# Moving the V loads of five batches from the SP queue to the ACT queue in a fused attention and feed-forward kernel

## The chip, the cores and the metric

The kernel runs on one core of a Trainium2 chip. The metric is the device time of one execution in microseconds (us). Each execution also lists its span and the mean granted TensorE clock (1.0 is full speed). The engines are PE (TensorE), DVE (VectorE), ACT (ScalarE), POOL (GpSimd) and SP (SyncE). "SPq" and "ACTq" in the profile are the instruction streams in which SP and ACT issue their DMAs.

## The reference, cut to what matters

```python
# q, k, v: (8 batches, 8 heads, 576 tokens, 64), f32
scores = scale * q @ k.T                       # per batch and head
mask   = (pos_q - pos_k >= 0) & (pos_q - pos_k < 64)   # causal window of 64
x      = softmax(where(mask, scores, -1e9)) @ v
x      = x.transpose(0, 2, 1, 3).reshape(4608, 512)
h      = x @ w_in                              # 512 -> 2048
g      = h * clip(h + 3, 0, 6) / 6             # hardswish
out    = g @ w_out                             # 2048 -> 512, f32
```

## The kernel before: the parts that matter

The 4608 tokens are handled in nine blocks, T0 to T8, of 512. A block has a first product (x times w_in, then a ReLU on ACT and a multiply on DVE, which make `gT`) and a second product (`gT` times w_out). The attention of batch T+1 is interleaved with the second product of block T. A batch also needs DMAs: loads of q, k and V, two transposing DMAs that make `QKT` (which I call the QKT transposes), and four that make `xT` (the x transposes). All of them, and the stores, are issued by SP:

```python
def load_v(b):                       # five DMAs: four of 256 KB, a tail of 128 KB, rows of 256 bytes
    ...
        nc.sync.dma_start(out=st, in_=v[b, h0 : h0 + nh, kb * P : kb * P + ss, :].rearrange("h s d -> s h d"))
    ...                              # POOL casts each piece to bf16
def load_nat(b):                     # batches 2 to 7
    ...
    nc.sync.dma_start_transpose(out=QK_tiles[...]..., in_=n[:]...)      # QKT <- nat, twice per batch
    ...
    for it in load_v(b):             # V follows q and k, on SP
        yield from it
...
    nc.sync.dma_start_transpose(out=xT[:, g, ...], in_=cell["o"][:]...) # xT <- opg, four per batch
```

The first product has three PSUM slots. A slot is free again when ACT and DVE have read it:

```python
for c in range(NCH):                              # eight chunks of two 128-column groups
    hT = two_banks([("g", T, c)])                 # waits until the DVE multiply of an earlier chunk is done
    ...matmuls into hT...
    nc.scalar.activation(out=t1[:], in_=hT[:], func=RELU, bias=half[:], scale=1.0 / 6.0)
    nc.vector.scalar_tensor_tensor(out=gT[...], in0=t1, scalar=1.0, in1=hT[:], op0=MIN, op1=MULT)
```

The matmuls beside which a unit of attention is put are given by a table (`S` is scores, `PV` is probabilities times V):

```python
REST = ((4, "S", 0), (11, "S", 1), (18, "S", 2), (19, "PV", 0), (25, "S", 3), (26, "PV", 1),
        (33, "PV", 2), (41, "PV", 3))
```

The softmax here doesn't subtract the row's maximum and nothing guards it: scores larger than these inputs give would overflow.

## Time and profile before

317.3 us, median of three runs (317.08 to 318.01). The profiled run has a span of 316.7 us.

The first lines are from the page of the kernel before: the busy table (us, share of the span, instructions), the DMA queues (packets, MB, share of 16 engines), and the DMA issues (KB each, median us from issue to landing).

```profile
PE 300.6 (95%) x2494; PEld 158.1 (50%) x2531; DVE 171.6 (54%) x201; ACT 165.4 (52%) x220; POOL 93.0 (29%) x133
...
q1 hardware_dynamic: 152784, 57.95, 84.4%
...
st<-in_v_dram SPq DMA_DIRECT2D x28, 256.0 KB, 5.0
...
QKT<-nat SPq DMA_TRANSPOSE x12, 5.5
```

PE is busy nearly all the time. One queue, SP's, carries 57.95 of the 58.35 MB.

Where PE is not busy after the opening, the view of waits tells why (us in total, times, longest):

```profile
PE ps L638 <- DMA xT<-opg: 1.9, 3, 0.7
```

L638 is the first product; it waits for x transposes. The windows view compares block T2, which has no such wait, with T4 (window, PE busy, PEld, DVE, ACT, POOL busy, then granted clock, DMA share, GB/s). Blocks are counted in this document from their first matmul of the first product:

```profile
94.13:126.24 32.11, 31.79 (x237) 15.80 (x240) 18.73 (x20) 17.80 (x24) 11.03 (x15) 1.00 1.14 205
158.51:192.20 33.69, 32.05 (x236) 15.82 (x240) 18.41 (x20) 17.80 (x24) 10.33 (x15) 1.00 0.99 197
```

T4 is 1.58 us longer, with about the same work. The timelines of SP and of PE around its start (start us, us, engine, line, operation, out<-in, count, then idle time before and its releaser) show the cause:

```profile
152.00 2.60 SPq L590 DMA_TRANSPOSE xT<-opg  x2
154.69 0.53 SPq L702 DMA_DIRECT2D out_dram<-osb  x1
155.32 3.98 SPq L590 DMA_TRANSPOSE xT<-opg  x2
...
160.02 6.52 SPq L374 DMA_TRANSPOSE QKT<-nat  x2
```

```profile
158.51 0.59 PE L638 MATMUL ps<-xT,win 128*128 128x512 bf16 x2
159.79 0.38 PE L638 MATMUL ps<-xT,win 128*128 128x512 bf16 x1 [0.69 <-DMA xT<-opg]
160.74 0.81 PE L638 MATMUL ps<-xT,win 128*128 128x512 bf16 x2 [0.58 <-DMA xT<-opg]
```

The last x transposes leave SP only at 155 to 159 us, and the first product wants them from 158.5 us.

### The profile page before, as it was taken

How to read it: one execution, taken by the hardware profiler on the slowest of the kernel's cores; microseconds unless marked ns; L12 is line 12 of the kernel's file. 1: busy time of each engine (PE TensorE's matmuls, PEld its weight loads, DVE VectorE, ACT ScalarE, POOL GpSimd, SP SyncE). 2: the span in 40 equal slices, each digit the busy share in tenths (PEclk: the TensorE clock that was granted, in tenths of full speed). 3: DMA queues.
4: the chain of work that ended last, by engine and by line, in shares of the span. 5: the costliest groups of instructions: out<-in, count | busy, mean ns of one | idle time of the engine just before them, and what ended most of it. 6: DMA issues, size and time to landing. Idle time of an engine off the chain costs nothing.

```text
span 316.7 us, 6130 instructions
## 1 busy us (share of the span) xinstructions
PE 300.6 (95%) x2494; PEld 158.1 (50%) x2531; DVE 171.6 (54%) x201; ACT 165.4 (52%) x220; POOL 93.0 (29%) x133
## 2 busy tenths in 40 slices
PE   6889979999999999999989999999999999999994
PEld 2554345544544455875534454445575544444442
DVE  5676568656825783477337751767166716404700
ACT  5655557367715771667146833683368336316511
POOL 3258738413730363037301640066003000000000
PEclk9999999999999999999999999999999999999998
DMA  8999999999999999999999989999993430010011
GB/s 212 240 370 386 386 307 214 235 214 209 211 202 196 218 214 192 198 207 214 178 184 221 202 188 165 240 206 197 204 213 58 126 91 0 33 68 33 0 68 67
DMA packets 152813, 58.35 MB, mean 184 GB/s; under 512 B 142032, under 2 KB 142032, under 8 KB 152784
## 3 DMA queue, kind: packets, MB, share of 16 engines
q1 hardware_dynamic: 152784, 57.95, 84.4%
q8 instruction: 20, 0.33, 0.4%
q14 instruction: 9, 0.07, 0.1%
HBM read 36.70 MB, written 9.44 MB: 146 GB/s over the span
## 4 chain that ended last, share of the span: by engine, by line
PE 77%; DMA 12%; SPq 6%; issue 1%; POOL 1%; DVE 0%; ACT 0%; ACTq 0%
PE ps L638 35%; PE acc L682 34%; DMA st<-in_moe_w_in_dram 4%; PE ps L528 4%; DMA st<-in_v_dram 3%; DMA st<-in_k_dram 3%; SPq L354 3%; PE ps L565 3%; PE ps L570 2%; DMA xT<-opg 2%; SPq L590 1%; SPq L316 1%; POOL V L261 1%; POOL win L261 1%; PE ps L607 0%
## 5 line engine op out<-in xcount | busy, mean ns | idle before, releaser
L650 DVE SCALAR_TENSOR_TENSOR gT<-t,ps 128x1024 bf16<-128x1024 bf16 x72 | 87.9, 1221 | 94.1 <-ACT t L647 94.1
L682 PE MATMUL acc<-wout,gT 128*128 128x512 bf16 x550 | 131.5, 379 | 2.3 <-issue 0.8
L638 PE MATMUL ps<-xT,win 128*128 128x512 bf16 (+4 forms) x693 | 126.1, 340 | 2.5 <-DMA xT<-opg 1.9
L647 ACT ACTIVATE t<-ps,half 128x1024 bf16<-128x1024 f32 x72 | 80.2, 1114 | 52.2 <-PE ps L638 52.2
L638 PEld LDWEIGHTS <-win 128*128 128x128 bf16 x704 | 65.2, 98 | 62.1 <-issue 2.9
L682 PEld LDWEIGHTS <-gT 128*128 128x128 bf16 x576 | 52.8, 98 | 58.5 <-issue 1.1
L699 ACT COPY osb<-acc 128x512 f32<-128x512 f32 x36 | 21.2, 590 | 69.6 <-PE acc L682 65.6
L537 ACT ACTIVATE pT<-ps 128x768 bf16<-128x768 f32 x64 | 48.6, 809 | 10.7 <-PE ps L528 10.4
L261 POOL CAST V<-st 128x512 bf16<-128x512 f32 (+1 forms) x30 | 19.4, 648 | 112.2 <-DMA st<-in_v_dram 108.8
L261 POOL CAST nat<-st 128x512 bf16<-128x512 f32 x48 | 37.3, 781 | 20.6 <-DMA st<-in_k_dram 11.7
L548 DVE TENSOR_TENSOR pT<-pT,mask 128x1920 bf16<-128x1920 bf16 x28 | 34.4, 1228 | 8.7 <-ACT pT L543 8.7
L583 DVE TENSOR_TENSOR opg<-ps,rec 128x640 bf16<-128x640 f32 x32 | 26.4, 825 | 1.1
L565 PEld LDWEIGHTS <-pT 128*128 128x128 bf16 x320 | 20.6, 98 | 5.3 <-DVE pT L548 0.2
L565 PE MATMUL ps<-V,pT 128*128 128x65 bf16 x320 | 22.0, 194 | 0.5 <-issue 0.3
L570 PE MATMUL ps<-V,pT 128*128 128x65 bf16 x256 | 20.9, 193 | 0.0
L528 PEld LDWEIGHTS <-QKT 64*128 64x128 bf16 x320 | 11.4, 94 | 14.4 <-issue 11.6
L570 PEld LDWEIGHTS <-pT 128*128 128x128 bf16 x256 | 17.9, 98 | 0.3 <-issue 0.3
L528 PE MATMUL ps<-QKT 64*128 64x192 bf16 (+1 forms) x320 | 17.7, 234 | 0.0
L580 DVE RECIPROCAL rec<-ps 128x10 f32<-128x10 f32 x32 | 7.0, 218 | 12.4 <-PE ps L570 12.1
L497 PE MATMUL ps<-ident,run 64*64 64x64 bf16 x288 | 6.7, 194 | 4.6 <-DVE run L258 2.8
L258 DVE CAST run<-st 128x576 bf16<-128x576 f32 x13 | 6.1, 473 | 8.1 <-DMA st<-in_q_dram 6.0
L261 POOL CAST nat<-tl 64x512 bf16<-64x512 f32 x12 | 9.3, 776 | 3.0 <-DMA tl<-in_q_dram 2.5
(46 smaller groups left out, 83.8 us busy)
## 6 DMA issues: line engine op xcount, KB each, us to landing
out_dram<-osb SPq DMA_DIRECT2D x36, 256.0 KB, 2.7
st<-in_v_dram SPq DMA_DIRECT2D x28, 256.0 KB, 5.0
st<-in_q_dram SPq DMA_DIRECT2D x24, 256.0 KB, 5.3
st<-in_k_dram SPq DMA_DIRECT2D x24, 256.0 KB, 5.4
st<-in_moe_w_in_dram SPq DMA_DIRECT2D x4, 1024.0 KB, 10.0
st<-in_moe_w_out_dram SPq DMA_DIRECT2D x4, 1024.0 KB, 14.8
st<-in_q_dram SPq DMA_DIRECT2D x8, 288.0 KB, 6.6
st<-in_k_dram SPq DMA_DIRECT2D x8, 288.0 KB, 5.8
```

Source lines behind the costliest of these rows:

```text
L261: return lambda s: nc.gpsimd.tensor_copy(out=out_ap, in_=in_ap) and None
L528: nc.tensor.matmul(st[:, h, off : off + w], lhsT=KT[h * D : (h + 1) * D, kb * P : (kb + 1) * P], rhs=QT[h * D : (h + 1) * D, kb * P : kb * ...
L537: nc.scalar.activation(out=pT[:, :, kbs[0] : kbs[0] + 2, 0:QW], in_=st[:, :, 0 : 2 * QW].rearrange("p h (k w) -> p h k w", k=2), func=EXP, ...
L548: pl.op("DVE", t, 1.2, lambda s: nc.vector.tensor_tensor(out=pT[:, :, :, 0:QW], in0=pT[:, :, :, 0:QW], in1=mask[:].rearrange("p (h k) w -> ...
L565: nc.tensor.matmul(ob, lhsT=pT[:, h, qb, 0:P], rhs=V[:, qb, 2 * g + h, :], start=True, stop=(qb == 0),)
L570: nc.tensor.matmul(ob, lhsT=pT[:, h, qb - 1, P : 2 * P], rhs=V[:, qb - 1, 2 * g + h, :], start=False, stop=True,)
L583: nc.vector.tensor_tensor(out=opg[:].rearrange("p k h d -> p h k d"), in0=ov[:, :, :, 0:D], in1=rec[:].unsqueeze(3).to_broadcast([P, 2, KB ...
L638: nc.tensor.matmul(hT[:, j, dst : dst + w], lhsT=win16[:, g, fc * P : (fc + 1) * P], rhs=xT[:, g, src : src + w], start=(g == 0), stop=(g ...
L647: nc.scalar.activation(out=t1[:], in_=hT[:], func=RELU, bias=half[:], scale=1.0 / 6.0)
L650: nc.vector.scalar_tensor_tensor(out=gT[:, 2 * c : 2 * c + 2, :], in0=cell["t"][:], scalar=1.0, in1=hT[:], op0=MIN, op1=MULT,)
L682: nc.tensor.matmul(accs[ts], lhsT=gT[:, fc, ts * P : (ts + 1) * P], rhs=wout16[:, fc, :], start=(fc == 0), stop=(fc == NFC - 1),)
L699: nc.scalar.copy(out=osb[:], in_=acc)
```

## The change

Its intent: take the five V loads of each of the batches 3 to 7 off SP, so that SP reaches the x transposes earlier. They go to ACT, spaced between its ReLUs, with a staging buffer of their own (`vstage`, `vtail`). That costs one of the six common staging buffers and one of three buffers for tails. The diff has more than that: it also rewrites the opening (order of loads and of attention units of batch 0, casts of the weights), takes the PV units earlier, and lets the first chunk of a block take its last x group last. Its core:

```diff
-NSTAGE = 6
+NSTAGE = 5
+VGAP = 1.4
+VISSUE = 0.6
...
+def stream_v(b):
+    def issue(kb):
+        def fn(s):
+            ...
+            nc.scalar.dma_start(
+                out=st.rearrange("p (h d) -> p h d", h=H),
+                in_=v[b, :, kb * P : kb * P + ss, :].rearrange("h s d -> s h d"))
+            ...
+            if kb < KB - 1:
+                pl.op("ACT", s + VGAP, VISSUE, issue(kb + 1))
+        return fn
+    gate = (("pv", b - 2, NG - 1), ("x", b - 1, NG - 1))   # in the plan, behind the x transposes of the batch ahead
+    pl.op("ACT", 0.0, VISSUE, issue(0), deps=gate)
...
 def load_nat(b):
     ...
-    for it in load_v(b):
-        yield from it
...
+        if c == 0:        # first chunk: the last x group last
+            order.sort(key=lambda x: x[2] == NG - 1 and x[1] is parts[-1])
...
-REST = ((4, "S", 0), (11, "S", 1), (18, "S", 2), (19, "PV", 0), (25, "S", 3), (26, "PV", 1),
-        (33, "PV", 2), (41, "PV", 3))
+REST = ((4, "S", 0), (10, "S", 1), (16, "S", 2), (17, "PV", 0), (22, "S", 3), (23, "PV", 1),
+        (29, "PV", 2), (36, "PV", 3))
... (opening: ORDER, MERGE, load_v_halves, split of the first w_in tile)
```

`pl` is a plan that is made when the program is built: it only sets the order of the instructions on each engine.

More of the change, by code (lines that the diff above doesn't have):

```diff
@@ L25 @@
 NEG = -30000.0
-QK_ENG = ([('ACT',), ('DVE',), ('ACT',), ('DVE',)], (("DVE", "ACT"),) * 4)
-X_ENG = ([('DVE', 'ACT'), ('DVE', 'ACT'), ('ACT',), ('DVE',)], (("DVE", "ACT"),) * 4)
+QK_ENG = ((('DVE', 'ACT'), ('ACT',), ('ACT',), ('ACT',)), (("DVE", "ACT"),) * 4)
+MERGE = ('ppppvvvppvpvpvvvvv', "ppppppvpvpvvv")
+ORDER = (('T', 0), ('T', 1), ('S0', 0), ('S1', 0), ('S1', 1), ('T', 2), ('S0', 1), ('PV', 0), ('S1', 2), ('T', 3), ('S0', 2), ('PV', 1), ('S1', 3), ('PV', 2), ('S0', 3), ('X', 0), ('PV', 3), ('X', 2), ('X', 1), ('X', 3))
+X_ENG = ((('DVE',), ('DVE', 'ACT'), ('DVE',), ('DVE', 'ACT')), (("DVE", "ACT"),) * 4)
 NWARM = 11
-PRIO = lambda g, f: ({"S0": 0, "S1": 0, "T": 1, "PV": 2, "X": 3}[f], g)
 class Plan:
@@ L137 @@
     stage = ctx.enter_context(tc.tile_pool(name="stage", bufs=NSTAGE))
-    tails = ctx.enter_context(tc.tile_pool(name="tails", bufs=3))
+    tails = ctx.enter_context(tc.tile_pool(name="tails", bufs=2))
+    vstage = ctx.enter_context(tc.tile_pool(name="vstage", bufs=1))
+    vtail = ctx.enter_context(tc.tile_pool(name="vtail", bufs=1))
     small = ctx.enter_context(tc.tile_pool(name="small", bufs=3))
@@ L187 @@
     P_ring = [consts.tile([P, 2, KB, 2 * P], BF16, name=f"pT{i}") for i in range(NPT)]
-    V_ring = [consts.tile([P, KB, H, VW], BF16, name=f"V{i}") for i in range(2)]
+    V_ring = [consts.tile([P, NG, KB, 2, VW], BF16, name=f"V{i}") for i in range(2)]
     nc.vector.memset(idle[:], 0.0)
@@ L234 @@
     for i, t in enumerate(V_ring):
-        at("POOL", 2.0 + 14 * i, 0.3, lambda t=t: nc.gpsimd.memset(t[:, :, :, D:VW], 1.0))
-        at("POOL", 2.2 + 14 * i, 0.9, zero("POOL", t[D:P, KB - 1, :, 0:D]), ("Vz", i))
+        at("POOL", 2.0 + 14 * i, 0.3, lambda t=t: nc.gpsimd.memset(t[:, :, :, :, D:VW], 1.0))
+        at("POOL", 2.2 + 14 * i, 0.9, zero("POOL", t[D:P, :, KB - 1, :, 0:D]), ("Vz", i))
     for t in natural:
         at("POOL", 17.0, 0.6, zero("POOL", t[S % P : P, :, KB - 1, :]))
-    dma = {"t": 2.4}
+    dma = {"t": 2.2, "lag": 0.2}
     DEPTH = 4.0
@@ L252, in moved @@
         dma["t"] = max(dma["t"], now) + kb / rate
-        land = dma["t"] + 1.9
+        land = dma["t"] + 1.9 + dma["lag"]
         return max(now + 0.06, dma["t"] - 5.0), land
@@ L281, in load_items @@
             if b < NR6:
-                yield from load_pairs(b)
+                ps, vs = load_pairs(b), load_v_halves(b) if b == 0 else load_v(b)
+                for c in MERGE[b]:
+                    yield next(ps if c == "p" else vs)
             else:
                 yield from load_nat(b)
+                if b == NR6:
+                    yield from load_v(b)
             if b == 0:
@@ L301, in tail_slot @@
         tail_hist.append(casts)
-        return tuple(tail_hist[-4]) if len(tail_hist) > 3 else ()
+        return tuple(tail_hist[-3]) if len(tail_hist) > 2 else ()
     def load_pairs(b):
-        vs = load_v(b)
         for gg in range(0, NG, 2):
@@ L319, in go @@
                         )
-                        fr, land = moved(s, 295, 385)
+                        fr, land = moved(s, 295, 385 if b else 330)
                         casts(("cast", b, i, g), land, [
@@ L324, in load_pairs @@
                     yield b, deps[i], go
-            if b == 0:
-                yield from next(vs)
-        for it in vs:
-            yield from it
     def load_v(b):
@@ L333, in load_v @@
         tiles = {}
-        nh = 4 if b == 0 else H
-        deps = stage_slot([("cast", b, 2, i, h0) for i in range(KB - 1) for h0 in range(0, H, nh)])
-        if b >= 2:
-            deps += (("pv", b - 2, NG - 1),)
-        if b == 2:
-            deps += (("issued", b, 1),)
-        if b > 2:
-            deps += (("s1v", b - 1),)
-        tdeps = tail_slot([("cast", b, 2, KB - 1, h0) for h0 in range(0, H, nh)])
-        for h0 in range(0, H, nh):
-            its = []
+        deps = stage_slot([("cast", b, 2, i) for i in range(KB - 1)])
@@ new lines, in load_v, with go @@
+        if b >= NR6:
+            deps += (("pv", b - 2, NG - 1), ("issued", b, 1))
+        tdeps = tail_slot([("cast", b, 2, KB - 1)])
+        for kb in range(KB):
+            ss = min(P, S - kb * P)
+            def go(s, kb=kb, ss=ss):
+                if kb == 0:
+                    tiles["t"] = stage.tile([P, 4, H * D], F32, name="st", tag="st")
+                if kb == KB - 1:
+                    st = tails.tile([P, H * D], F32, name="tl", tag="tl")[:ss, :]
+                else:
+                    st = tiles["t"][:, kb, :]
+                nc.sync.dma_start(
+                    out=st.rearrange("p (h d) -> p h d", h=H),
+                    in_=v[b, :, kb * P : kb * P + ss, :].rearrange("h s d -> s h d"),
+                )
+                fr, land = moved(s, 262 * ss / P, 205)
+                casts(("cast", b, 2, kb), land, [(
+                    ("POOL",), V[:ss, :, kb, :, 0:D], st.rearrange("p (g h d) -> p g h d", g=NG, h=2), H * D)])
+                return fr
+            yield b, deps + tdeps if kb == KB - 1 else deps, go
@@ new lines, in stream_v @@
+    def stream_v(b):
+        V = V_ring[b % 2]
+        tiles = {}
+        def issue(kb):
+            ss = min(P, S - kb * P)
+            def fn(s):
+                if kb == 0:
+                    tiles["t"] = vstage.tile([P, 4, H * D], F32, name="sv", tag="sv")
+                if kb == KB - 1:
+                    st = vtail.tile([P, H * D], F32, name="tv", tag="tv")[:ss, :]
+                else:
+                    st = tiles["t"][:, kb, :]
+                nc.scalar.dma_start(
+                    out=st.rearrange("p (h d) -> p h d", h=H),
+                    in_=v[b, :, kb * P : kb * P + ss, :].rearrange("h s d -> s h d"),
+                )
+                _, land = moved(s, 262 * ss / P, 205)
+                casts(("cast", b, 2, kb), land, [(
+                    ("POOL",), V[:ss, :, kb, :, 0:D], st.rearrange("p (g h d) -> p g h d", g=NG, h=2), H * D)])
+                if kb < KB - 1:
+                    pl.op("ACT", s + VGAP, VISSUE, issue(kb + 1))
+            return fn
+        gate = (("pv", b - 2, NG - 1), ("x", b - 1, NG - 1))
+        if b > NR6 + 1:
+            gate += tuple(("cast", b - 1, 2, kb) for kb in range(KB))
+        pl.op("ACT", 0.0, VISSUE, issue(0), deps=gate)
@@ L345, in load_v, with load_v_halves, go @@
+    def load_v_halves(b):
+        V = V_ring[b % 2]
+        tiles = {}
+        deps = stage_slot([("cast", b, 2, i, kb) for i in range(2) for kb in range(KB - 1)])
+        tdeps = tail_slot([("cast", b, 2, i, KB - 1) for i in range(2)])
+        for i in range(2):
             for kb in range(KB):
                 ss = min(P, S - kb * P)
-                def go(s, kb=kb, ss=ss, h0=h0):
-                    if "t" not in tiles:
-                        tiles["t"] = stage.tile([P, 4, H * D], F32, name="st", tag="st")
-                    if kb == KB - 1 and "l" not in tiles:
-                        tiles["l"] = tails.tile([P, H * D], F32, name="tl", tag="tl")
-                    st = tiles["l"][:ss, :] if kb == KB - 1 else tiles["t"][:, kb, :]
-                    st = st[:, h0 * D : (h0 + nh) * D].rearrange("p (h d) -> p h d", h=nh)
+                def go(s, i=i, kb=kb, ss=ss):
+                    if not tiles:
+                        tiles["t"] = stage.tile([P, 2, 4, 4 * D], F32, name="st", tag="st")
+                        tiles["l"] = tails.tile([P, 2, 4 * D], F32, name="tl", tag="tl")
+                    st = tiles["l"][:ss, i, :] if kb == KB - 1 else tiles["t"][:, i, kb, :]
@@ L354, in go @@
                     nc.sync.dma_start(
-                        out=st,
-                        in_=v[b, h0 : h0 + nh, kb * P : kb * P + ss, :].rearrange("h s d -> s h d"),
-                    )
-                    fr, land = moved(s, 262 * ss / P * nh / H, 200)
-                    eng = ("DVE", "ACT", "POOL") if b == 0 else ("POOL",)
-                    casts(("cast", b, 2, kb, h0), land, [(eng, V[:ss, kb, h0 : h0 + nh, 0:D], st, nh * D)])
-                    return fr
-                its.append((b, deps + tdeps if kb == KB - 1 else deps, go))
@@ L363, in load_v @@
-            yield its
+                        out=st.rearrange("p (h d) -> p h d", h=4),
+                        in_=v[b, 4 * i : 4 * i + 4, kb * P : kb * P + ss, :].rearrange("h s d -> s h d"),
+                    )
+                    fr, land = moved(s, 131 * ss / P, 200)
+                    casts(("cast", b, 2, i, kb), land, [(
+                        ("DVE", "ACT", "POOL"), V[:ss, 2 * i : 2 * i + 2, kb, :, 0:D],
+                        st.rearrange("p (g h d) -> p g h d", g=2, h=2), 4 * D)])
@@ L365, in load_nat @@
+                    return fr
+                yield b, deps + tdeps if kb == KB - 1 else deps, go
     def load_nat(b):
@@ L408, in load_nat, with go @@
                 yield b, deps + tail_slot([("cast", b, i, kb)]) if kb == KB - 1 else deps, go
-        for it in load_v(b):
-            yield from it
     WC = FF // 4
     def load_w():
+        dma["lag"] = 0.8
         for i in range(4):
             deps = stage_slot([("win", i, 0), ("win", i, 1)])
-            def go(s, i=i):
-                st = stage.tile([P, NG, WC], F32, name="st", tag="st")
-                nc.sync.dma_start(
-                    out=st[:],
-                    in_=moe_w_in[:, i * WC : (i + 1) * WC].rearrange("(g p) f -> p g f", p=P),
-                )
-                fr, land = moved(s, 1049, 388)
-                for hf in range(2):
-                    casts(("win", i, hf), land, [(
-                        ("POOL",), win16[:, 2 * hf : 2 * hf + 2, i * WC : (i + 1) * WC],
-                        st[:, 2 * hf : 2 * hf + 2, :], 1024)])
-                return fr
-            yield 0, deps, go
+            n = 2 if i == 0 else 1
+            tiles = {}
+            for j in range(n):
+                def go(s, i=i, j=j, n=n, tiles=tiles):
+                    w, w2 = WC // n, WC // 2
+                    if not tiles:
+                        tiles["t"] = stage.tile([P, n, NG, w], F32, name="st", tag="st")
+                    st = tiles["t"][:, j]
+                    nc.sync.dma_start(
+                        out=st, in_=moe_w_in[:, i * WC + j * w : i * WC + (j + 1) * w].rearrange("(g p) f -> p g f", p=P),
+                    )
+                    fr, land = moved(s, 1049 / n, 388 if n == 1 else 350)
+                    for hf in range(2) if n == 1 else (j,):
+                        c0 = i * WC + hf * w2
+                        casts(("win", i, hf), land, [(
+                            ("POOL",) if i else ("DVE", "ACT", "POOL"), win16[:, :, c0 : c0 + w2],
+                            st[:, :, hf * w2 : (hf + 1) * w2] if n == 1 else st, NG * w2)])
+                    return fr
+                yield 0, deps, go
         for i in range(4):
@@ L474, in ready @@
         elif f == "PV":
-            ks = [soft(b, g)] + vcasts(b, g)
+            ks = soft(b, g) + vcasts(b, g)
         else:
@@ L481, in soft @@
     def soft(b, g):
-        return ("mask", b, g) if b else ("exp", b, g, 1)
+        return [("mask", b, g)] if b else [("exp", b, g, i) for i in range(2)]
     def vcasts(b, g):
-        nh = 4 if b == 0 else H
-        return [("cast", b, 2, kb, 2 * g // nh * nh) for kb in range(KB)]
+        return [("cast", b, 2, g // 2, kb) for kb in range(KB)] if b == 0 else [("cast", b, 2, kb) for kb in range(KB)]
     def tqk(b, g):
@@ L556, in pv @@
     def pv(b, g):
-        for r in [soft(b, g)] + vcasts(b, g):
+        for r in soft(b, g) + vcasts(b, g):
             pl.wait(r)
@@ L565, in pv @@
                 nc.tensor.matmul(
-                    ob, lhsT=pT[:, h, qb, 0:P], rhs=V[:, qb, 2 * g + h, :],
+                    ob, lhsT=pT[:, h, qb, 0:P], rhs=V[:, g, qb, h, :],
                     start=True, stop=(qb == 0),
@@ L570, in pv @@
                     nc.tensor.matmul(
-                        ob, lhsT=pT[:, h, qb - 1, P : 2 * P], rhs=V[:, qb - 1, 2 * g + h, :],
+                        ob, lhsT=pT[:, h, qb - 1, P : 2 * P], rhs=V[:, g, qb - 1, h, :],
                         start=False, stop=True,
@@ L629, in s1 @@
         for c in range(NCH):
-            if T == 0 and c % 2 == 0:
-                pl.wait(("win", c // 2, 0))
-                pl.wait(("win", c // 2, 1))
+            if T == 0:
+                pl.wait(("win", c // 2, c % 2))
             hT = two_banks([("g", T, c)])
-            for j in range(2):
-                fc = 2 * c + j
-                for dst, src, w in parts:
-                    for g in range(NG):
-                        nc.tensor.matmul(
-                            hT[:, j, dst : dst + w], lhsT=win16[:, g, fc * P : (fc + 1) * P],
-                            rhs=xT[:, g, src : src + w], start=(g == 0), stop=(g == NG - 1),
-                        )
-                pl.pe(4 * 0.216)
+            order = [(j, p, g) for j in range(2) for p in parts for g in range(NG)]
+            if c == 0:
+                order.sort(key=lambda x: x[2] == NG - 1 and x[1] is parts[-1])
+            for j, (dst, src, w), g in order:
+                nc.tensor.matmul(
+                    hT[:, j, dst : dst + w], lhsT=win16[:, g, (2 * c + j) * P : (2 * c + j + 1) * P],
+                    rhs=xT[:, g, src : src + w], start=(g == 0), stop=(g == NG - 1),
+                )
+                pl.pe(0.216 * w / TB)
             cell = {}
@@ L711 @@
     next_load(0.0)
+    for b in range(NR6 + 1, B):
+        stream_v(b)
     warm = two_banks(["warm"])
@@ L728, in unit @@
             xt(b, g, cells.pop((b, g)))
-    todo = {g: ["T", "S0", "S1", "PV", "X"] for g in range(NG)}
-    while any(todo.values()):
-        for g, f in sorted(((g, u[0]) for g, u in todo.items() if u), key=lambda x: PRIO(*x)):
-            if ready(f, 0, g):
-                todo[g].pop(0)
-                unit(f, 0, g)
-                break
-        else:
-            pl.pe(0.05)
+    for f, g in ORDER:
+        unit(f, 0, g)
     for r in held.pop():
```

## The prediction

> **What bounds the kernel now.** TensorE: 300.6 of 316.7 us busy (busy table), 77% of the chain of waits. By the windows view, a 512-token block with attention beside it (T1 from 62.2 us, T2 from 94.3) takes 32.1 us with 31.7 busy; nothing can be won there. The loss is elsewhere:
> - T3 and T4 take 33.4 and 33.2 us. The timeline shows TensorE waiting for "DMA xT<-opg": 0.69 + 0.57 us from 159.1, 0.63 at 193.0. SP's timeline shows why: SP is full all block: two QKT transposes 6.6 us, five V loads 5.5, q 5.7, k 5.5 to 7.2, stores, four x transposes of 1.2. In T3 the k loads end at 151.2 us and the x transposes issue only from 152.0 to 159.3 (one took 2.66 us).
> - The opening (0 to 62.2 us) has about 8 us of TensorE idle: 5 before the first feed-forward matmul at 22.5 us, 3 in T0, of which 0.4 for a w_out cast and 1.6 for the first q/k casts of batch 1. From 16 to 40 us DMA moves about 386 GB/s (slices), so T0's weights and the q/k after them come no earlier.
>
> **What the change does** (the diff has more than its title).
> 1. For batches 3 to 7, V's issues (5.5 us) leave SP for ACT. SP gets slack, so x transposes no longer stand behind k. The bytes stay. [...]
> 2. A block's last PV moves from the 42nd to the 37th matmul of the second product: 5 x 0.216 = 1.1 us more for the x transposes; the first chunk also takes its last x group last. Estimate: the 1.9 us of x stalls go, and 0.5 of small slips.
> 3. In T0, 22 rather than 14 second-product matmuls precede batch 1's transposes: 8 x 0.216 = 1.7 us of waiting filled. The opening is reordered and the first w_in tile split: 0.3 to 1 us by estimate, partly lost again in a longer wait for w_out. One staging buffer fewer may delay batch 1's k and V by 1 us.
> 4. Added: 25 ACT issues, 0.57 us each [...], three per block between ReLUs. ReLU 1.11 + 0.57 = 1.68 us, just under a chunk's 1.73 us: no stall. At 1.1 us [...] ACT falls 0.5 us behind per chunk, mostly absorbed by three PSUM slots.
>
> **Prediction.** 317.3 - 2.4 (T3, T4) - 1.9 (opening) + 0.3 (ACT) = 313.3 us; 310.8 to 316.8. Faster by over 2%: 0.13; within: 0.79; slower: 0.08.
>
> **What would show it.** T3 and T4 near 32.1 us without waits for xT; SP free before x; ACT's issues near 0.6 us, ReLU not late; T0 ending near 60 us; T1, T2 unchanged.
>
> **What would make it wrong.** ACT held in its issue: [...] V now falls beside the QKT transposes, 3.3 us each on SP. If ACT waited that long, five blocks would lose 1 to 3 us each. Or V, sharing bandwidth, lands too late for PV.

The 0.216 us of a matmul is a first product without waits, 13.81 us, over its 64 matmuls. The 0.57 us and the 1.1 us of an ACT issue were estimates from V's issues on SP in the trace before: their median is 0.58 us there, and from T1 on they take 0.40 to 2.07 us, 0.95 in the mean. (The five of a block take 4.4 to 5.2 us there, not 5.5.)

The prediction counts its blocks from a slightly later point: the waits at 159.1 and 193.0 us, which it puts into T3 and T4, stand in this document at the starts of T4 and T5.

## The result, and the profile after

The changed kernel takes **328.73 us** (median of 4 runs, 326.47 to 330.39), the kernel before 317.43 us in the same rounds. The ratio is 1.0349, with a 95% interval of 1.0283 to 1.0416: slower by 3.5%. Executions over 1.5% slower than the fastest of the same kernel are left out of the means. A ratio here and below is the mean time of one kernel's fast runs over that of the other's of the same rounds, so it is not quite the ratio of the medians that are quoted. The prediction of 313.3 us (310.8 to 316.8) was wrong.

The page of the kernel after, the same parts:

```profile
PE 306.8 (94%) x2531; PEld 158.8 (49%) x2531; DVE 172.1 (53%) x204; ACT 164.9 (51%) x218; POOL 91.0 (28%) x132
...
q1 hardware_dynamic: 129872, 52.05, 72.9%
q10 hardware_dynamic: 23440, 5.90, 9.6%
...
sv<-in_v_dram ACTq DMA_DIRECT2D x20, 256.0 KB, 5.3
...
QKT<-nat SPq DMA_TRANSPOSE x12, 9.0
```

V is on its own queue (q10). V lands nearly as fast as before, but a QKT transpose now lands after 9.0 us instead of 5.5.

The starts of the first products, from the PE timelines of both profiled runs, tell where the time came from:

| block | before: start, length us | after: start, length us | difference |
|---|---|---|---|
| opening and T0 | 0, 62.03 | 0, 63.52 | +1.49 |
| T1 | 62.03, 32.10 | 63.52, 32.14 | +0.04 |
| T2 | 94.13, 32.11 | 95.66, 34.92 | +2.81 |
| T3 | 126.24, 32.27 | 130.58, 36.28 | +4.01 |
| T4 | 158.51, 33.69 | 166.86, 33.45 | -0.24 |
| T5 | 192.20, 32.89 | 200.31, 34.70 | +1.81 |
| T6 to the last matmul | 225.09, 87.69 | 235.01, 87.69 | 0.00 |

Of the 9.9 us, 1.5 lie in the opening and T0. The rest lies in T2, T3 and T5, and in T4 a new loss has taken the place of the old one; all of this is in the first products. PE's waits after (only the two that matter here; L690 is the first product now):

```profile
PE ps L690 <- DVE gT L702: 5.8, 3, 2.4
PE ps L690 <- DMA xT<-opg: 2.3, 3, 1.3
```

The first wait did not exist before: PE finds no free PSUM slot, because a ReLU and so the DVE multiply behind it are late. It occurs in T3, T4 and T5. ACT's timeline at the start of T3 shows the late ReLU. The lines are, in order: V's third and fourth piece, two ReLUs, V's tail, three ReLUs.

```profile
130.85 0.37 ACTq L374 DMA_DIRECT2D sv<-in_v_dram  x1
...
132.53 0.37 ACTq L374 DMA_DIRECT2D sv<-in_v_dram  x1
134.27 1.11 ACT L699 ACTIVATE t<-ps,half 128x1024 bf16<-128x1024 f32 x1 [0.63 <-PE ps L690]
138.57 0.61 ACTq L374 DMA_DIRECT2D tv<-in_v_dram  x1
139.23 3.13 ACT L699 ACTIVATE t<-ps,half 128x1024 bf16<-128x1024 f32 x3 [3.84 <-DMA QKT<-nat]
```

The issues themselves are cheap: 0.37 us, and beside the ReLU. But nothing starts on ACT between 134.27 and 138.57 us, and what ended the idle time is "DMA QKT<-nat", a transposing DMA on the *other* queue. SP and PE at the same time:

```profile
128.38 10.23 SPq L423 DMA_TRANSPOSE QKT<-nat  x2
```

```profile
130.58 8.90 PE L690 MATMUL ps<-xT,win 128*128 128x192 bf16 x80
141.65 4.53 PE L690 MATMUL ps<-xT,win 128*128 128x192 bf16 x25 [2.18 <-DVE gT L702]
```

PE goes on until its three slots are full, stalls for 2.2 us, and resumes when the third chunk's ReLU and multiply are done. The records of line L374 from 126 to 142 us (duration in ns: minimum, median, maximum; then the first and last start) hold the wait itself:

```profile
L374 ACTq EVENT_SEMAPHORE  x3: 17/38/4251, 127.3 to 134.3; - x3
L374 ACTq DMA_DIRECT2D tv<-in_v_dram x1: 614/614/614, 138.6 to 138.6; - x1
```

A semaphore wait of 4.25 us in ACT's stream, the last of three, from 134.3 to 138.6 us: that is the gap. The wait is a record of its own, and the tail's record, 0.61 us long, follows it. So ACT waited here for a semaphore. It was not held within its issue, which is what I had named as my main worry.

T3 lost 4.0 us, but its stall was 2.2. The rest is the clock. The windows view (the third number from the end is the granted clock):

```profile
142.00:144.00 2.00, 2.00 (x14) 1.47 (x12) 1.86 (x2) 0.36 (x1) 0.61 (x1) 0.63 1.20 289
144.00:146.00 2.00, 2.00 (x11) 1.39 (x10) 0.39 (x1) 1.11 (x1) 0.72 (x2) 0.52 1.37 218
146.00:148.00 2.00, 2.00 (x21) 1.70 (x20) 0.83 (x1) 0.99 (x1) 1.11 (x2) 1.00 1.37 217
```

Right after the stall the trace has a clock record of 0.50 from 142.52 us, 3.41 us long: by estimate from the windows, 2 x (1 - 0.63) + 2 x (1 - 0.52) = 1.7 us more. So PE's busy time rose by more than the work did (a part of the rise in the busy table is only that the trace before lacks 37 of 2531 matmul records).

### The profile page after: what moved, and what is told of

Its sections match the earlier page's. It is cut to its first block, busy times and chain, and to the rows that moved or that the text cites. A ratio compares the mean times of both kernels' runs of the same rounds, so it can differ in the third digit from the quotient of the medians.

```text
span 326.5 us, 6180 instructions
## 1 busy us (share of the span) xinstructions
PE 306.8 (94%) x2531; PEld 158.8 (49%) x2531; DVE 172.1 (53%) x204; ACT 164.9 (51%) x218; POOL 91.0 (28%) x132
## 2 busy tenths in 40 slices
DMA packets 153341, 58.35 MB, mean 179 GB/s; under 512 B 142048, under 2 KB 143072, under 8 KB 153312
## 4 chain that ended last, share of the span: by engine, by line
PE 72%; DMA 20%; SPq 2%; POOL 2%; DVE 2%; ACT 1%; issue 1%; ACTq 0%; POOLq 0%
PE acc L734 34%; PE ps L690 29%; PE ps L581 4%; DMA st<-in_moe_w_out_dram 4%; DMA st<-in_moe_w_in_dram 3%; DMA sv<-in_v_dram 3%; DMA st<-in_k_dram 3%; DMA QKT<-nat 3%; PE ps L618 3%; PE ps L623 2%; DMA tl<-in_v_dram 2%; DVE gT L702 1%; DMA xT<-opg 1%; ACT t L699 1%; SPq L351 1%; POOL wout L266 1%
## 5 line engine op out<-in xcount | busy, mean ns | idle before, releaser
L734 PE MATMUL acc<-wout,gT 128*128 128x512 bf16 x576 | 136.9, 380 | 1.9 <-POOL wout L266 1.5
L690 PE MATMUL ps<-xT,win 128*128 128x512 bf16 (+4 forms) x704 | 128.9, 344 | 8.2 <-DVE gT L702 5.8
L690 PEld LDWEIGHTS <-win 128*128 128x128 bf16 x704 | 66.1, 99 | 69.7 <-issue 9.7
L266 POOL CAST nat<-st 128x512 bf16<-128x512 f32 x48 | 34.8, 729 | 25.2 <-DMA st<-in_q_dram 15.7
L601 DVE TENSOR_TENSOR pT<-pT,mask 128x1920 bf16<-128x1920 bf16 x28 | 35.5, 1269 | 6.4 <-ACT pT L596 6.4
L266 POOL CAST V<-sv 128x512 bf16<-128x512 f32 x20 | 12.4, 619 | 73.7 <-DMA sv<-in_v_dram 71.2
L263 DVE CAST run<-st 128x576 bf16<-128x576 f32 x15 | 7.6, 515 | 10.8 <-DMA st<-in_q_dram 6.2
L265 ACT COPY QKT<-ps 128x1152 bf16<-128x1152 bf16 x6 | 6.8, 1129 | 11.2 <-PE ps L550 11.2
L266 POOL CAST V<-st 128x512 bf16<-128x512 f32 (+1 forms) x10 | 6.2, 626 | 21.3 <-DMA st<-in_v_dram 21.3
L266 POOL CAST nat<-tl 64x512 bf16<-64x512 f32 x12 | 10.9, 910 | 1.5 <-DMA tl<-in_q_dram 0.8
```

Source lines behind the costliest of these rows:

```text
L266: return lambda s: nc.gpsimd.tensor_copy(out=out_ap, in_=in_ap) and None
L601: pl.op("DVE", t, 1.2, lambda s: nc.vector.tensor_tensor(out=pT[:, :, :, 0:QW], in0=pT[:, :, :, 0:QW], in1=mask[:].rearrange("p (h k) w -> ...
L690: nc.tensor.matmul(hT[:, j, dst : dst + w], lhsT=win16[:, g, (2 * c + j) * P : (2 * c + j + 1) * P], rhs=xT[:, g, src : src + w], start=(g ...
L734: nc.tensor.matmul(accs[ts], lhsT=gT[:, fc, ts * P : (ts + 1) * P], rhs=wout16[:, fc, :], start=(fc == 0), stop=(fc == NFC - 1),)
```

## Why ACT waits: the theory and its rivals

**Theory A: the two queues share eight completion semaphores.** Each DMA record of the trace names the semaphore that its DMA signals. In the kernel before, the 201 DMA issues of SP name eight, strictly in turn. In the kernel after there are 177 issues on SP and 25 on ACT. They name the same eight, and only one way of merging the two streams keeps the eight in turn throughout. That is the program order: the eight go round *whichever engine issues*. The rotation is made when the program is built. In both traces each DMA is issued only after the DMA that last held its semaphore, the one eight before it, has landed: the shortest distance is 0.016 us, over 193 and 194 issues. With all DMAs on SP, from T1 on, that one had landed at least 2.8 us earlier. With two streams, ACT can meet a DMA of SP that is still under way. The DMAs of T3 in the merged order, from the records (number, counted from 0, engine, operation, output, semaphore signalled, and the semaphores waited for; cut):

```
104 SP   DMA_TRANSPOSE QKT  signals 101
105 ACT  DMA_DIRECT2D sv    signals 104
106 SP   DMA_TRANSPOSE QKT  signals 105
...
112 ACT  DMA_DIRECT2D tv    signals 101   waits 101 (DMA 104), 110 (DMA 103), 99 (POOL)
```

The wait of 4.25 us is for 101 and 110. DMA 103, a store, had landed at 131.28 us, before that wait began; DMA 104 had not. The tail of V in T3 (112) is eight behind the first QKT transpose (104). The same holds in T4 (137 behind 129) and T5 (162 behind 154), but not in T2 or T6. These are exactly the three blocks with the wait for `gT`. The times fit as well: in T3 the first QKT transpose was issued at 128.38 us and landed 10.1 us later, at 138.5; the tail's record begins at 138.57. In T4 the pair is 173.6 and 173.73 us, in T5 208.3 and 208.39. The landing in T3 (the view of line L423 from 128.3 to 130 us), then SP and ACT in T4:

```profile
L423 SPq DMA_TRANSPOSE QKT<-nat x1: 4664/4664/4664, 128.4 to 128.4; - x1
DMA to landing us min/median/max: 10.1/10.1/10.1
...
164.65 10.03 SPq L423 DMA_TRANSPOSE QKT<-nat  x2
173.73 0.61 ACTq L374 DMA_DIRECT2D tv<-in_v_dram  x1
```

T3 alone could not tell the landing of the first transpose from the end of SP's second issue, which came at 138.6 us too (128.38 + 10.23). T4 can: SP was issuing until 174.7 us, and ACT's tail left at 173.73, right after the landing.

In T2 it is SP that waits: the last x transpose of batch 2 (DMA 78) is eight behind the first V load of batch 3 (DMA 70), which is on ACT. That load landed at 96.09 us, and the transpose was issued at 96.15. The wait view of SP between 90 and 100 us has it, and PE pays for it when it needs that x:

```profile
SPq L643 <- DMA sv<-in_v_dram: 0.9, 1, 0.9
```

```profile
99.74 1.46 PE L690 MATMUL ps<-xT,win 128*128 128x512 bf16 x6 [1.27 <-DMA xT<-opg]
```

This is only a part of T2's loss. PE also waited 0.27 and 0.75 us there for x transposes that stood behind no V load. The four x transposes landed 3.2 to 4.2 us after their issue, against 2.6 to 3.5 in the kernel before, where no V load was in flight beside them.

**Rival B:** V on ACT collides with the transposing DMAs themselves, in the issue or in the transfer, whatever the semaphores. Then moving V away from ACT helps, and changing the numbering alone does not. **Rival C:** the loss comes from the rest of the diff: the opening, the earlier PV, five buffers instead of six.

## The experiments

Nine kernels ran. All gave correct results, and each was compared with the kernel before in its own rounds. "First product" below means the length of that part of a block in the profiled run: 13.81 to 13.98 us where PE does not stop.

### 1. V back on SP, the rest of the change kept

```diff
-    for b in range(NR6 + 1, B):
-        stream_v(b)
...
     yield from load_nat(b)
-    if b == NR6:
-        yield from load_v(b)
+    yield from load_v(b)
... (vstage and vtail gone; load_v waits for what it waited for in the kernel before)
```

> The changed kernel with V of batches 3 to 7 back on the SP queue and in the common staging buffers; opening, block order and five staging buffers as in the changed kernel. Theory A (the V loads on ACT are the cause, through waits that the two queues impose on each other) and rival B (V on ACT is the cause, through DMA contention alone) both expect T2 to T5 free of ReLU waits, first products of 14 us, and about 317 us (315.5 to 318.5). Rival C (the rest of the diff is the cause) expects it to stay above 323 us.

Measured: 318.27 us (318.13 to 318.6), ratio 1.0036 [1.0000, 1.0072]. The first products of T2 to T5 are 14.04, 13.97, 14.36 and 13.96 us. Without V on ACT nearly the whole loss is gone, so rival C falls. But the rest of the change gains nothing either.

### 2. The same with six staging buffers

```diff
-NSTAGE = 5
+NSTAGE = 6
```

> As e1, with six staging buffers as before instead of five. If the fifth-buffer limit is what made T0's second product 1.7 us longer (27.4 against 25.7 us), this is 1 to 2 us faster than e1: about 315.5 us. If the reordered opening itself is the cause, it equals e1 within 0.5 us.

Measured: 317.21 us (316.13 to 318.36), ratio 1.0002 [0.9957, 1.0046]. In the profiled run T1 starts at 60.57 us, against 62.96 with five buffers. In the timed runs the sixth buffer is worth about 1 us, within their scatter. Equal to the kernel before.

### 3. Only the numbering changed: one tiny SP load ahead of V's tail

The kernel after, with a 1 KB load on SP put before V's tail of batches 4, 5 and 6. It has no use but to count: it moves the tail to the ninth place behind the QKT transpose.

```diff
+    if kb == KB - 1 and 4 <= b <= 6:
+        nc.sync.dma_start(out=dummy[:], in_=v[b, 0, 0:16, 0:16])
     if kb == KB - 1:
         st = vtail.tile([P, H * D], F32, name="tv", tag="tv")[:ss, :]
```

> The changed kernel plus one 1 KB dummy load on the SP queue ahead of the last V load of batches 4, 5 and 6. It shifts the round robin of the eight DMA completion semaphores by one, so that this V load on ACT no longer waits for the landing of the first QKT transpose. Theory A expects the ReLU waits of 2.2, 1.2 and 2.4 us in T3, T4 and T5 to vanish, the QKT transposes to stay near 10 us for two, and about 321 us (319.5 to 323). Rival B [...] expects no change: 327 to 330 us with the same waits.

Measured: 319.87 us (318.52 to 320.98), ratio 1.0083 [1.0037, 1.0129]. The first products of T3, T4 and T5 are 13.98, 13.81 and 13.82 us; that of T2, which was left as it was, 16.69. Three extra DMAs made the kernel faster by 8 to 9 us (the kernel after ran in other rounds; the two ratios to the kernel before are 1.0349 and 1.0083). The start of T3 on ACT, then SP's transposes:

```profile
131.65 0.38 ACTq L377 DMA_DIRECT2D sv<-in_v_dram  x1
133.39 1.11 ACT L702 ACTIVATE t<-ps,half 128x1024 bf16<-128x1024 f32 x1 [0.63 <-PE ps L693]
133.47 1.83 ACTq L377 DMA_DIRECT2D tv<-in_v_dram  x1
135.34 1.11 ACT L702 ACTIVATE t<-ps,half 128x1024 bf16<-128x1024 f32 x1 [0.84 <-PE ps L693]
```

```profile
127.52 9.96 SPq L426 DMA_TRANSPOSE QKT<-nat  x2
```

The tail is now issued at 133.47 us, in the middle of the same pair of transposes (10 us, as slow as in the kernel after), and the ReLU follows at 135.34. The issue is longer, 1.83 us, so there is something of rival B in it, but the PSUM slots absorb it. The longest semaphore wait of these ACT issues falls from 4251 ns to 38:

```profile
L377 ACTq EVENT_SEMAPHORE  x3: 17/38/38, 126.4 to 133.4; - x3
```

Such a record is good evidence when it is long, but a short one does not exclude a wait: in T4 and T5 of the kernel after it is 38 ns too, and begins only when the transpose has landed. What decides here is that the tail leaves at 133.47 us, before the first transpose (issued at 127.52) lands, 10.0 us after its issue.

The transposes did not change, V did not change, only the number did: for T3 to T5, A holds and B falls as the cause of the loss. T2 was not tested here.

### 4. The kernel before with V on ACT alone

`stream_v` in the kernel before, with five staging buffers, two for tails, and nothing else of the diff. Here the order of DMAs happens to put no V load of T3 to T5 eight behind a QKT transpose; the meeting of x and V in T2 remains.

```diff
-NSTAGE = 6
+NSTAGE = 5
+for b in range(NR6 + 1, B):
+    stream_v(b)
... (load_v(b) in load_nat only for b == NR6)
```

> The kernel before with only the V loads of batches 3 to 7 moved to ACT (own staging buffer, five common ones). In its built program no V load shares a semaphore with a QKT transpose, but one x transpose of batch 2 shares one with the first V load, as in the changed kernel. Theory A expects no ReLU wait in T3 to T5, an x wait of 1 to 2.5 us at the start of T2, and 317 to 321 us. Rival B expects ReLU waits as in the changed kernel and 324 to 328 us, since the same transfers stand beside the same transposes.

Measured: 323.61 us (321.19 to 324.57), ratio 1.0213 [1.0167, 1.026], classed as unclear at 2%. The waits are where A puts them: first products of T3 to T5 are 13.97, 14.34 and 14.35 us, that of T2 is 18.90. The one exception is small: PE waits 0.4 us for `gT` in T5, where a V issue of 1.97 us on ACT and the tail's wait for an earlier V piece of its own queue come together. The time missed A's range of 317 to 321 us and is nearly in B's (324 to 328), so here only the waits speak for A. The size of T2's loss was the error: 3.08 us of idle time, and then, as in T3 of the kernel after, a half clock (0.76 from 97 to 100 us, 0.50 from 100 to 102), which by estimate, 3 x (1 - 0.76) + 2 x (1 - 0.50), is another 1.7 us. Nor was the profiled run typical: it was the fastest, with a mean clock of 0.995, and the other three had 0.984 to 0.988. The semaphore explains 2.0 us of T2's wait (SP stood so long for a V load); the last x transpose then took 3.8 us to land, against 2.6 in the kernel before.

### 5. Control: the same tiny loads where they change nothing

The kernel after, with the three loads right behind the last x transpose of batches 3 to 5, so that both the QKT transpose and the tail move by one, and the distance stays eight.

```diff
+    if g == NG - 1 and 3 <= b <= 5:
+        nc.sync.dma_start(out=dummy[:], in_=v[b, 0, 0:16, 0:16])
     fr, land = moved(s, 164, 230)
```

> Control to e3: the same three dummy loads in the changed kernel, but issued right behind the fourth x transpose, ahead of the QKT transposes. The last V load is then still eight DMAs behind the first QKT transpose. Theory A expects the changed kernel's time (326 to 330 us) and its ReLU waits of 1 to 2.5 us in T3 to T5. If the dummy loads helped in some other way (a pause on the SP queue, another alignment), this should fall to about 320 us like e3.

Measured: 331.82 us (326.99 to 333.13). Two of the four runs were slow; they are in this median but not in the ratio, and the two fast ones took 326.99 and 331.42 us. Ratio 1.0327 [1.0215, 1.044]. The first products of T3 to T5 are 15.68, 15.15 and 18.44 us. PE's wait for `gT` is there as in the kernel after:

```profile
PE ps L693 <- DVE gT L705: 5.5, 3, 2.8
```

As slow as the kernel after: the tiny loads as such do not help.

### 6. Both meetings avoided in the kernel after

The third kernel, and V of batch 3 one gate later, so that no x transpose of batch 2 is eight behind it.

```diff
+    if b == NR6 + 1:
+        gate += (("s1x", b - 1),)       # 0.4 us after the start of block b - 1, in the plan
... (the mark "s1x" itself)
```

> e3 with the V loads of batch 3 emitted one accumulator copy later, so that the first no longer stands eight DMAs ahead of the last x transpose of batch 2. Theory A (x transpose held for that load's landing, then flying beside it) expects T2's first product to go from 16.7 to about 14 us and 317.3 us (316 to 318.5). If T2's wait came from the x transposes being late anyway (SP backlog), it stays at 16 us or more and the time at 320.

Measured: 321.43 us (318.15 to 322.39), ratio 1.0065 [0.9993, 1.0138]; expected was about 317.3: a miss. The first product of T2 is down from 16.69 to 14.93 us, but its second product went from 18.30 to 20.90. A wait of 1.5 us for a QKT transpose and one of 0.9 us for a cast of V are in it, which the third kernel does not have there. So the x wait went, and most of it came back as late QKT. No semaphore held those two transposes: SP issued each about 0.1 us after the end of its instruction before. They landed 10.1 and 11.5 us after their issue, against 8.3 and 9.8 in the third kernel. ACT also stood longer in its issue here than in any other kernel:

```profile
101.44 2.44 ACTq L377 DMA_DIRECT2D sv<-in_v_dram  x1
```

The tail then waited for the second V piece, eight places before it on ACT's own queue, and PE waited 0.6 us for `gT`. So a part of this block's loss may be what rival B names. The later gate also moves V's traffic away from the x transposes, so this experiment and the next cannot tell how much of T2's loss is the semaphore and how much is that traffic.

### 7. Both meetings avoided in the kernel before

The same gate in the fourth kernel.

> e4 (kernel before, V of batches 3 to 7 on ACT) with the same delay of batch 3's V loads. No V load or transpose on one queue then waits for a slow DMA on the other. Theory A: T2 falls from 18.9 to about 14 us; 316 us (314.5 to 317.5), equal to or up to 1% faster than the kernel before, its waits for x in T3 and T4 reduced. Rival B: above 319 us.

Measured: 318.58 us (318.24 to 318.92), ratio 0.9997 [0.9937, 1.0057]. The time is above the range of 314.5 to 317.5 us, but the kernel before took 319.2 us in these rounds; against it the seventh kernel is equal, the least that A expected. The first products of T2 to T5 are 13.81, 13.98, 14.56 and 14.36 us. V is on ACT for five batches, the QKT transposes land late (a median of 9.2 us), and the kernel costs nothing more than the kernel before. It also gains nothing.

### 8. A meeting made on purpose

The seventh kernel, with the same three tiny loads as in the third. In *this* order of DMAs they move the fourth V load to the eighth place behind the first QKT transpose (111 behind 103, 137 behind 129, 163 behind 155).

> e7 plus the same three 1 KB dummy loads as in e3, which here shift the rotation so that the fourth V load of batches 4, 5 and 6 does share its semaphore with the first QKT transpose. Theory A expects the ReLU waits of 1 to 2.5 us in T3, T4 and T5 to appear in a kernel that had none, and 5 to 9 us more than e7: 321 to 326 us. Rival B expects e7's time, within 1 us.

Measured: 323.84 us (322.56 to 325.3), ratio 1.016 [1.0099, 1.0222], classed as unclear at 2%; in the same rounds it is 5 us slower than the seventh kernel. The first products of T3 to T5 are 15.11, 14.66 and 18.40 us. ACT at T5, then SP, then PE's waits:

```profile
199.05 1.11 ACT L685 ACTIVATE t<-ps,half 128x1024 bf16<-128x1024 f32 x1 [0.61 <-PE ps L676]
204.09 0.38 ACTq L385 DMA_DIRECT2D sv<-in_v_dram  x1
204.52 1.11 ACT L685 ACTIVATE t<-ps,half 128x1024 bf16<-128x1024 f32 x1 [4.35 <-PE ps L676]
```

```profile
193.68 10.38 SPq L411 DMA_TRANSPOSE QKT<-nat  x2
```

```profile
PE ps L676 <- DVE gT L688: 3.7, 2, 2.7
```

The V load leaves at 204.09 us, and the ReLU behind it starts only then. The profile puts this idle time down to "PE ps", but PE had long written that slot; releasers are inferred, and this one is wrong. The same tiny loads that made one kernel faster by 8 to 9 us make this one slower by about 5. In T4 ACT's wait was short (the load left at 168.63 us) and cost nothing that shows. A load of the size, place and queue of these three cannot do both; the distance in the rotation can.

### 9. Only the earlier PV and the order of the first chunk

The kernel before with two small parts of the diff: `REST` as in the change, and the last x group last in the first chunk. V stays on SP, with six buffers.

> The kernel before with two parts of the change alone: the earlier positions of scores and PV beside the second product, and the last x group taken last in the first chunk of a block. V stays on the SP queue, six staging buffers, the opening as before. My prediction's second term, taken alone: the 1.9 us of x waits at the starts of T4 and T5 go (first products 13.9 to 14.2 us long instead of 15.40 and 14.60), and the time falls by 1.5 to 2.4 us, to 315.0 to 316.0 us: within 2%, but an interval that excludes 1 if runs scatter no more than the kernel before does. Rival (what the runs that hold these parts, with V on SP, showed: no gain): the time stays within 0.5 us of the kernel before, because the waits come back later in the block, as a wait for the QKT transposes or for V.

Measured: 316.7 us (316.05 to 317.77, 6 runs) against 318.05 us (11 runs), ratio 0.9961 [0.993, 0.9992]. That is 0.4% or 1.2 us by the ratio: a small gain. The median is 0.7 us above the range I gave. From the start of T1 to that of T6 the profiled run takes 161.21 us against 163.06 before, 1.85 us less. PE has no wait for x any more, and from 162 to 195 us, the rest of T4 and the start of T5, it is full:

```profile
162.00:195.00 33.00, 33.00 (x245) 16.15 (x244) 18.70 (x20) 18.52 (x25) 10.64 (x15) 1.00 1.12 209
```

The rival (the waits come back later) does not show in the profile, and the interval excludes 1. This is the best ratio of all the kernels here, and it has no V on ACT. Why the timed runs gain less than the profile is not shown. The opening may hide a part: this edit does not touch it, and it still differed by 1.2 us between the two profiled runs (T1 starts at 63.23 us here, at 62.03 before).

## Why the prediction was wrong, point by point

- **"What bounds the kernel now": right.** PE was the limit, and the 1.9 us of waits for x were real: the last experiment got 1.85 us of them back.
- **Term 1, "SP gets slack, so x transposes no longer stand behind k": right for T4 and T5, wrong for T2.** There, the last x transpose got a new wait, for a V load on ACT, and all four landed later against the start of the block. The bytes stayed (58.35 MB in both profiled runs), and V's landing time nearly did (5.0 and 5.3 us). V's issues left SP's stream, but that was not what needed relief: the small edit of the last experiment removed the waits with V on SP.
- **Term 2, the earlier PV and the first chunk: right, and the only part that paid.** Its 2.4 us (1.9 of x waits, 0.5 of slips) measured 1.85 in the profile, and 1.2 us by the ratio. In the kernel after it was buried.
- **Term 3, the opening, -1.9 us: not there.** T1 began 1.5 us later, not 1.9 earlier. Over all profiled runs T1 starts at 62.4 to 63.5 us with the new opening and five buffers, at 60.6 in one with six, and at 61.3 to 64.0 with the old opening. These ranges overlap, so what the new opening is worth stays open; it is not 1.9 us with five buffers.
- **Term 4, "25 ACT issues ... no stall", +0.3 us: this is the step that failed.** It costed the issue, and the issue was even cheaper than I said (0.37 us, beside the ReLU). What it left out is what the issue *waits for*. ACT's program order makes each ReLU wait behind the V load ahead of it, and that load waits for a DMA of SP's queue because the two share a rotation of eight semaphores. The term measured, as the difference of the first products between the kernel after and the third experiment: 4.0 us in T3 (17.98 and 13.98), 1.3 in T4 (15.13 and 13.81), 2.6 in T5 (16.40 and 13.82), 7.9 us in all and not 0.3 (the half clock behind T3's stall is in it). The same sharing in the other direction held SP for 0.9 us in T2; how much of T2's 2.8 us is due to it, and how much to V's traffic beside the x transposes, is not shown.
- **A loss that no term had: the clock.** In T3 of the kernel after, the stall of 2.18 us was followed by a granted clock of 0.63 and then 0.52, each over 2 us, which by estimate nearly doubled its price (1.7 us more). It was not always so: after the stall of 2.43 us in T5 of the same run the clock stayed at 1.00. What decides it is not shown.
- **A price of V on ACT that no term had: the QKT transposes land later.** The median is 5.5 us in the kernel before and 9.0, 9.3 and 9.2 us in the kernel after, the third and the seventh, where V is on ACT. It cost little by itself: the seventh kernel has the time of the kernel before. Why they land later is not shown.
- **"What would make it wrong: ACT held in its issue": the right symptom, the wrong cause.** I expected the issue itself to be held beside the QKT transposes; that was a guess that no trace had shown. With the same V loads issued in the middle of the same transposes, but with another number in the rotation, the stall was gone. Where ACT's issue did meet the transposes it took up to 2.44 us. The three PSUM slots absorbed most of that: PE waits for `gT` of 0.4 to 0.6 us were left in single blocks of the fourth, sixth and seventh kernels, together with waits of the tail for V pieces of its own queue.

What stays open: why the QKT of one batch took so long to land in the sixth kernel, how T2's loss divides, and what the opening is worth.

## What to carry to other kernels

Before a DMA is moved to a compute engine's stream, ask not only what its issue costs but what it waits for, and list the built program's DMAs with their completion semaphores: where semaphores are shared in rotation, as here, a DMA on one queue can wait for a slow DMA on another (4.25 us on ACT in T3 of the kernel after), and what stands behind it in program order waits too (the ReLU, 3.84 us). A DMA that takes as long to land as the QKT transpose here (10.1 us) should not be the predecessor, in that rotation, of one on an engine that feeds the critical path; one harmless DMA more or less can decide that (three loads of 1 KB made one kernel 8 to 9 us faster, another about 5 us slower). And if only a few late transfers hurt, moving their consumer or their producer by a few matmuls may do what a second queue was meant to do: here it gained 1.2 us by the ratio, and V on ACT nothing.
